# Turning activation rows with VectorE's 32x32 transpose instead of TensorE, for five experts and two token chunks of a fused attention and mixture-of-experts kernel

## The chip, the cores and the metric

The kernel runs on one core of a Trainium2 chip. The metric is the device time of one execution in microseconds (us); each time below is a median of several executions or that of the one profiled execution, as said. The engines are PE (TensorE matmul; PEld its weight loads), DVE (VectorE), ACT (ScalarE), POOL (GpSimd) and SP (SyncE, which here issues most DMAs).

## The reference

```python
def reference(...):
    y = linear_attention(q, k, v, a_re, a_im)      # complex decay, 2 x 8 heads x 768 x 48
    x = y.transpose(0, 2, 1, 3).reshape(1536, 384)
    logits = x @ w_gate                            # 8 experts, top 1
    e, gate_w = argmax(logits, 1), softmax(logits)[argmax]
    # every token goes to a slot of its expert, at most 384 slots an expert
    h = relu(disp @ w1)                            # [8, 384, 384] x [8, 384, 1024]
    z = h @ w2                                     # x [8, 1024, 384]
    x = gate_w * z[expert, slot]                   # back in token order
    g = x @ w_in                                   # 384 x 2048
    g = max(g, 0) + alpha * min(g, 0)
    return g @ w_out                               # 2048 x 384
```

## The kernel before

Three stages follow one another. The attention stage (to about 152 us) is ordered by a planner written in Python; it ends by scattering every token's row of 384 numbers to its expert's slots in a DRAM buffer `xs_d`. The expert stage (about 152 to 300 us) runs the eight experts one after the other on 256 slots each. The chunk stage (about 300 to 503 us) runs the second network over 1536 tokens in three chunks of 512. An `If` at the end, not taken for these inputs, repeats experts that hold more than 256 tokens.

Each number is carried as two parts, a high part (`xh`, `wh`, `gh`) rounded by ScalarE and a low part (`xl`, `wl`, `gl`) that VectorE takes as the difference, and each product is three matmuls (high by high, high by low, low by high). `ffn` does the two layers for an expert or a chunk. It runs over blocks `ft` of 128 hidden units: 8 for an expert, 16 for a chunk. For each it issues nine matmuls into `hp` (L1234), has ACT and DVE make `gh` and `gl`, and issues the second layer's matmuls into `y` (L1217) one or more blocks later: six for an expert's two tiles of tokens, twelve for a chunk's four. In the first block of an expert or chunk the six matmuls that read `xh` come ahead of the three that read `xl`.

The first layer needs the rows turned: 384 features on partitions, tokens along the free axis. `split_rows` does that for 128 rows: three TensorE transposes of 128x128 into one PSUM tile `pt` (L1194), then `xh` from `pt` by ACT (L1196) and `xl` by DVE (L1197). For experts 1 to 7 `gather_expert` loads the rows of the next expert from `xs_d` by two DMAs on SP (L1297) and `split_expert` turns both blocks. For the second and third chunk `combine` gathers the rows of four tiles by indirect DMAs on POOL (L1364), multiplies them by the gate (L1370) and turns them. The first chunk has a path of its own (`first_chunk`), and expert 0 too.

Work for what comes next is hung on hooks of the running `ffn`: a hook of block `ft` is called in the program after that block's `gh` and `gl`. `GA` and `HK1` say at which block rows are gathered, `GS[e]` at which block of expert e those of expert e + 1 are turned (3 in experts 1 to 6, 5 in expert 0). In a chunk gathering and turning share one hook: block 9 in the first chunk, 3 in the second. `follow` puts an instruction behind the block's last `gl` (for DVE) or its `hp` (for PE) on its own engine. The order of each engine's queue is otherwise chosen by the tile framework when it builds the program, from modelled times; every engine then runs its queue in order. Weights come in pieces: SP loads them into staging tiles, and hooks call `piece`, which makes `wh` (L359) and `wl` (L360). Buffers with the tag `rows` hold the gathered rows: four of 128x384 before. The output copies `o` of the chunks use them too.

Of the kernel before, what the change touches and what calls it, by code (L numbers as in the profile page):

```python
# [10 lines left out]
F32 = mybir.dt.float32  # L11
# [66 lines left out]
GATE = 18  # L78
BEHIND = ('A', 'AV')
GA = 1  # L80
GS = [5] + [3] * 6 + [7]
HK0 = 0
GATES_AT = 3
PAIRED = 15
# [135 lines left out]
def tile_kernel(  # L220
# [50 lines left out]
    xs_d = tc.dram_tile([NE * CAP, DM], F32, name="xs_d")  # L271
    ys_d = tc.dram_tile([NE * CAP + 1, DM], F32, name="ys_d")
    gs_d = tc.dram_tile([NE * CAP, 1], F32, name="gs_d")
    srel = cpool.tile([P, CHT], F32, name="srel")
    eidx = cpool.tile([P, CHT], U32, name="eidx")

# [25 lines left out]
    def land():  # L302
        for tag, todo in coming.items():
            while todo and busy[tag] < slots[tag]:
                kk, j0, k = todo[0]
                behind_rows = kk >= GATE or (kk == GATE - 1 and j0 >= 2)
                if (behind_rows and not first_gathers) or (kk == 3 and not second_rows):
                    break
                todo.pop(0)
                busy[tag] += 1  # L310
                src, c, n, m = shape(kk)
                rows = src[j0 * m * P:(j0 + k) * m * P, :]
                if kk >= 2 * NE:
                    st = swp.tile([P, m, n, 2], U32, tag="sw", name=f"sw{kk}", bufs=slots["sw"])
                    ins = nc.sync.dma_start(
                        out=st.rearrange("p m n w -> p m (n w)"), in_=rows.bitcast(U32).rearrange("(m p) n -> p m n", p=P)
                    )
                else:
                    p_ = stp if tag == "st" else swp
                    st = p_.tile([P, k * m, n], F32, tag=tag, name=f"st{kk}", bufs=slots[tag])  # L320
                    ins = nc.sync.dma_start(out=st, in_=rows.rearrange("(m p) n -> p m n", p=P))
# [12 lines left out]
                for j in range(k):  # L334
                    landed[kk, j0 + j] = (st[:, j * m:(j + 1) * m], tag, j == k - 1)
# [850 lines left out]
    def work(behind, limit):  # L1186
        if todo and todo[0][0] <= limit:
            piece(*todo.pop(0), behind)
        land()

    def split_rows(rows, xh, xl, j, behind=None):
# [12 lines left out]
    def ffn(xh, xl, N, units, sink, hooks, tail=None, ends="A", hold=0):  # L1204
# [67 lines left out]
        for t in range(nt):  # L1272
            if hold and t == nt - 1:
                for n, e in enumerate("VA"):
                    cs = slice(n * DM // 2, (n + 1) * DM // 2)
                    o = fp.tile([P, DM // 2], F32, tag="o", name="o", bufs=OB)
                    if e == "A":
                        A(out=o, in_=ys[t][:, cs], func=ACTF.Copy)
                    else:
                        V.tensor_copy(out=o, in_=ys[t][:, cs])  # L1280
                    sink(t, o, cs, nc.scalar if n else nc.sync)
                continue
            last_ones = len(ends) > 1
            o = fp.tile([P, DM], F32, tag="rows" if last_ones else "o", name="o", bufs=4 if last_ones else OB)
            if ends[t % len(ends)] == "A":
                A(out=o, in_=ys[t], func=ACTF.Copy)
            else:
                V.tensor_copy(out=o, in_=ys[t])
            sink(t, o)

    def gather_expert(e):
        xh = fp.tile([P, KC, SLOTS], F32R, tag="xh", name="xh")
        xl = fp.tile([P, KC, SLOTS], F32R, tag="xl", name="xl")
        rows = []
        for j in range(SLOTS // P):
            rows.append(fp.tile([P, DM], F32, tag="rows", name="rows", bufs=4))
            ins = nc.sync.dma_start(out=rows[j], in_=xs_d[e * CAP + j * P:e * CAP + (j + 1) * P, :])  # L1297
            after_scatters(ins)
            if e == 1:
                second_rows.append(ins)  # L1300
        return xh, xl, rows

    def split_expert(xh, xl, rows, behind):
        for j in range(SLOTS // P):
            split_rows(rows[j], xh, xl, j, behind)
        return xh, xl

    def fullest_expert(behind):
        ones = fp.tile([P, P], BF16, tag="rows", name="ones", bufs=4)
        cnt = fp.tile([P, NE], BF16, tag="rows", name="cnt", bufs=4)  # L1310
# [4 lines left out]
        mc = fp.tile([P, 1], F32, tag="rows", name="mc", bufs=4)  # L1315
        V.tensor_reduce(out=mc, in_=pc, axis=AX.X, op=ALU.max)
        V.tensor_copy(out=most, in_=mc)

    def overflow():
# [6 lines left out]
        with tc.If(fullest > SLOTS):  # L1326
            for e in range(NE):
                r0 = e * CAP + SLOTS
                rows = fp.tile([P, DM], F32, tag="rows", name="rows", bufs=4)
# [11 lines left out]
                for ft in range(FT):  # L1341
                    hp = pm.tile([P, P], F32, tag="h", name="hp", bufs=3)
                    for c in range(KC):
                        T.matmul(out=hp, lhsT=a1[c][:, ft * P:(ft + 1) * P], rhs=xT[:, c, :], start=(c == 0), stop=(c == KC - 1))
                    hr = fp.tile([P, P], F32, tag="gn", name="hr")
                    V.tensor_scalar(out=hr, in0=hp, scalar1=0.0, scalar2=None, op0=ALU.max)
                    a2 = fp.tile([P, DM], F32, tag="rows", name="a2", bufs=4)
                    nc.sync.dma_start(out=a2, in_=w2[e, ft * P:(ft + 1) * P, :])
                    T.matmul(out=yp, lhsT=hr, rhs=a2, start=(ft == 0), stop=(ft == FT - 1))
                o = fp.tile([P, DM], F32, tag="o", name="o", bufs=OB)  # L1350
                V.tensor_copy(out=o, in_=yp)
                nc.sync.dma_start(out=ys_d[r0:r0 + P, :], in_=o)
            for c in range(NTILE // CHT):
                ffn(*combine(c, CHT), CHT * P, [NE, NE + 1], lambda t, o, c=c: store_chunk(c, t, o), {})

    xe = (xh0, xl0)

    def combine(c, n, behind=None):
        xh = fp.tile([P, KC, n * P], F32R, tag="xh", name="xh")
        xl = fp.tile([P, KC, n * P], F32R, tag="xl", name="xl")  # L1360
        for j in range(n):
            i = c * n + j
            rows = fp.tile([P, DM], F32, tag="rows", name="rows", bufs=4)
# [55 lines left out]
    def first_chunk():  # L1419
# [4 lines left out]
        pts.append(pm.tile([P, n * P], F32, tag="tr", name="pt"))  # L1424
        got = []
        for j in range(n):
            rows = fp.tile([P, DM], F32, tag="rows", name="rows", bufs=4)
# [58 lines left out]
    for e in range(NE):  # L1486
# [11 lines left out]

        def turned(behind, e=e):
            if e + 1 < NE:  # L1500
                nxt[0] = split_expert(*nxt[0], behind)
            else:
                first_chunk_rows(behind, range(CHT // 2))

# [24 lines left out]
    for c in range(nch):  # L1529
# [52 lines left out]
```

## Time and profile before

| | |
|---|---|
| median of 3 runs | 513.21 us (512.49 to 513.21) |
| the profiled execution, whole | 511.71 us |
| its span (first to last instruction) | 509.6 us |
| granted TensorE clock, mean | 0.998 |

A row of a timeline gives start, duration, engine, line, operation, tiles and shape; `xN` at its end says that N instructions are merged, and a bracket gives the idle time of the engine ahead of it and what ended it. A matmul's duration there includes its way through the array, and matmuls overlap; what one takes of PE is the distance from its start to the next start.

### The profile page before, as it was taken

The page shows a single profiled execution, that of the slowest core. Times are in us where ns is not written, and L with a number is a line of the kernel's source. Part 1 is how long each engine was busy: PE and PEld are TensorE (multiplying, and loading weights), DVE is VectorE, ACT ScalarE, POOL GpSimd, SP SyncE. Part 2 cuts the span into 40 slices and gives each one's busy share as a digit, 9 for nine tenths or more (in the row PEclk, how much of TensorE's full clock was granted, in tenths as well). Part 3 has the DMA queues.
Part 4 walks back from the last instruction along what each step waited for, and adds up shares of the span by engine and source line. Part 5 has one row for each costly group of instructions (what it writes and reads, how often), then busy time and mean ns, then how long its engine had stood idle before and what let it go on. Part 6 is the DMA issues. An engine that isn't in the chain of part 4 may idle for free.

```text
span 509.6 us, 8757 instructions
## 1 busy us (share of the span) xinstructions
PE 496.0 (97%) x3379; PEld 452.4 (89%) x3379; DVE 343.7 (67%) x624; ACT 306.3 (60%) x566; POOL 75.0 (15%) x73
## 2 busy tenths in 40 slices
PE   7899999999999999999999999999999999999994
PEld 7778787888899999999999989999998999989984
DVE  5698999898956777767689769988354334333332
ACT  7898999989633755666663455556454344433441
POOL 0243045264431000300000330000030000000000
PEclk9999999999999999999999999999999999999999
DMA  8845789221234978859744475330030000100002
GB/s 266 274 134 172 238 282 342 87 93 41 93 127 153 381 227 292 222 177 360 268 146 150 147 271 187 131 123 1 0 125 0 1 0 1 62 2 0 1 0 68
DMA packets 38210, 71.96 MB, mean 141 GB/s; under 512 B 4777, under 2 KB 29362, under 8 KB 37394
## 3 DMA queue, kind: packets, MB, share of 16 engines
q1 hardware_dynamic: 36226, 66.12, 39.0%
q0 software_dynamic: 1792, 5.12, 3.1%
q8 instruction: 28, 0.46, 0.4%
q14 instruction: 20, 0.16, 0.1%
q10 hardware_dynamic: 144, 0.10, 0.1%
HBM read 56.76 MB, written 14.56 MB: 140 GB/s over the span
## 4 chain that ended last, share of the span: by engine, by line
PE 86%; ACT 6%; DVE 3%; DMA 2%; issue 0%; SPq 0%
PE hp L1234 32%; PE y L1217 32%; PE y L687 4%; PE sc L668 3%; PE u L701 2%; PE px L727 2%; PE pkT L648 2%; PE pt L1194 1%; PE pqT L648 1%; PE pt L560 1%; PE pl L509 1%; ACT L421 1%; PE pt L563 1%; DMA sw<-in_moe_w_out 1%; DMA ar<-in_a_re 1%; ACT w L492 1%
## 5 line engine op out<-in xcount | busy, mean ns | idle before, releaser
L1234 PE MATMUL hp<-xh,wh 128*128 128x256 f32 (+1 forms) x336 | 110.2, 330 | 0.0
L1234 PE MATMUL hp<-xh,wl 128*128 128x256 f32 (+1 forms) x336 | 109.6, 328 | 0.0
L1217 PE MATMUL y<-wh,gh 128*128 128x384 f32 x320 | 108.6, 339 | 0.0
L1217 PE MATMUL y<-wl,gh 128*128 128x384 f32 x320 | 107.7, 337 | 0.0
L1234 PE MATMUL hp<-xl,wh 128*128 128x256 f32 (+1 forms) x336 | 107.4, 330 | 0.1
L1217 PE MATMUL y<-wh,gl 128*128 128x384 f32 x320 | 91.7, 339 | 0.1
L360 DVE TENSOR_TENSOR wl<-st,wh 128x768 fp32r<-128x768 f32 (+1 forms) x63 | 67.4, 1070 | 17.5 <-ACT wh L359 16.9
L1251 DVE SCALAR_TENSOR_TENSOR gn<-gn,nalp,gp 128x512 f32<-128x512 f32 x48 | 35.9, 749 | 63.0 <-ACT gp L1250 62.1
L1249 ACT ACTIVATE gn<-hp 128x512 f32<-128x512 f32 x48 | 28.7, 598 | 81.0 <-PE hp L1234 76.5
L1234 PEld LDWEIGHTS hp<-xh,wh 128*128 128x128 f32 x336 | 63.2, 188 | 5.3 <-ACT xh L1482 0.6
L1234 PEld LDWEIGHTS hp<-xl,wh 128*128 128x128 f32 x336 | 62.2, 188 | 5.5 <-DVE xl L1483 0.6
L1234 PEld LDWEIGHTS hp<-xh,wl 128*128 128x128 f32 x336 | 63.2, 188 | 4.4
L359 ACT ACTIVATE wh<-st 128x768 fp32r<-128x768 f32 (+1 forms) x63 | 58.8, 933 | 8.1 <-DMA st<-in_moe_w 4.8
L1217 PEld LDWEIGHTS y<-wl,gh 128*128 128x128 f32 x320 | 60.2, 188 | 1.5
L1217 PEld LDWEIGHTS y<-wh,gh 128*128 128x128 f32 x320 | 60.2, 188 | 1.5
L1217 PEld LDWEIGHTS y<-wh,gl 128*128 128x128 f32 x320 | 56.8, 188 | 1.1 <-DVE gate L989 0.4
L1253 DVE TENSOR_TENSOR gl<-gn,gh 128x512 fp32r<-128x512 f32 x48 | 33.1, 691 | 29.6 <-ACT gh L1252 29.6
L1244 ACT ACTIVATE gh<-hp 128x256 fp32r<-128x256 f32 x64 | 24.5, 383 | 47.4 <-PE hp L1234 47.4
L455 POOL TENSOR_TENSOR ai<-ai 128x384 f32<-128x384 f32 x36 | 33.7, 936 | 65.8 <-ACT ai L512 64.0
L1252 ACT ACTIVATE gh<-gn 128x512 fp32r<-128x512 f32 x48 | 30.2, 629 | 19.5 <-DVE gn L1251 18.3
L1245 DVE SCALAR_TENSOR_TENSOR gl<-hp,gh 128x256 fp32r<-128x256 f32 x64 | 26.9, 421 | 13.5 <-ACT gh L1244 13.4
L1250 ACT ACTIVATE gp<-hp 128x512 f32<-128x512 f32 x48 | 28.4, 591 | 0.0
(178 smaller groups left out, 765.8 us busy)
## 6 DMA issues: line engine op xcount, KB each, us to landing
st<-in_moe_w SPq DMA_DIRECT2D x24, 512.0 KB, 3.8
st<-in_moe_w SPq DMA_DIRECT2D x12, 768.0 KB, 4.3
sw<-in_moe_w_in SPq DMA_DIRECT2D x6, 1024.0 KB
sw<-in_moe_w_out SPq DMA_DIRECT2D x8, 768.0 KB, 4.2
xs_d<-zero SPq DMA_DIRECT2D x4, 1152.0 KB
vt<-in_v SPq DMA_DIRECT2D x12, 256.0 KB
st<-in_moe_w SPq DMA_DIRECT2D x8, 384.0 KB, 3.4
ys_d<-o SPq DMA_DIRECT2D x16, 192.0 KB, 5.2
```

Of the source, the lines that this page charges most:

```text
L359: follow(A(out=wh[:, js], in_=st, func=ACTF.Copy), behind, "A")
L360: follow(V.tensor_tensor(out=wl[:, js], in0=st, in1=wh[:, js].bitcast(F32), op=ALU.subtract), behind, "V")
L455: (V if e == "V" else G).tensor_tensor(out=t, in0=t, in1=t, op=ALU.mult)
L1217: ins = T.matmul(out=ys[t], lhsT=a[:, sl], rhs=b[:, f, :], start=(ft == 0 and m == 0), stop=(ft == nf - 1 and m == 2))
L1234: ins = T.matmul(out=hp, lhsT=a[:, c, fs], rhs=b[:, c, :], start=(n == 0), stop=(n == 3 * KC - 1))
L1244: last["A"] = A(out=gh, in_=hp, func=ACTF.Relu)
L1245: last["V"] = V.scalar_tensor_tensor(out=gl, in0=hp, scalar=0.0, in1=gh.bitcast(F32), op0=ALU.max, op1=ALU.subtract)
L1249: A(out=gn, in_=hp, func=ACTF.Relu, scale=-1.0)
L1250: A(out=gp, in_=hp, func=ACTF.Relu)
L1251: V.scalar_tensor_tensor(out=gn, in0=gn, scalar=nalp[:, ft:ft + 1], in1=gp, op0=ALU.mult, op1=ALU.add)
L1252: last["A"] = A(out=gh, in_=gn, func=ACTF.Copy)
L1253: last["V"] = V.tensor_tensor(out=gl, in0=gn, in1=gh.bitcast(F32), op=ALU.subtract)
```

## The change

For experts 2 to 6 and for the second and third chunk the rows are turned by VectorE's transpose, which transposes every 32x32 block in place. The four blocks of a 128-column band must therefore already lie in the right group of 32 partitions, and the DMA that loads the rows does that. One VectorE transpose turns both 128-row blocks (128x768), one ACT instruction makes `xh` and one DVE instruction `xl`, from SBUF and not from PSUM.

For an expert (`blocked(..., True)`) four DMAs load 32 partitions each, in runs of 96 numbers (384 bytes). The 384 features are dealt out differently over the partitions for this, and the first-layer weights of these experts are loaded with rows in the same order (`first_rows`). For a chunk (`blocked(..., False)`) the gated rows are first stored to a new DRAM buffer `zs_d`, two tiles at a time, and loaded again in runs of 32 numbers (128 bytes). The `rows` tag now has two buffers of 128x2x384, the same bytes as before; `pair_tile` takes one, also for the tile that receives the transpose (`turned`).

Turning moves to block 5 of experts 1 to 5; expert 6 stays at 3. In the chunks it has a hook of its own, block 13 (`HK2`) of the first chunk and 8 of the second. Expert 1, expert 7 and the first chunk are turned by TensorE as before, and their rows come by one DMA for the pair.

```diff
-GS = [5] + [3] * 6 + [7]
+GS = [5] + [5] * 5 + [3, 7]
+DEALT = (2, 3, 4, 5, 6)
+HK2 = 13
+BLK = 32
+    def first_rows(src, k):
+        return src.rearrange("(p k) n -> k p n", k=DM // P)[k].unsqueeze(1)
...
+    def pair_tile(name):
+        return fp.tile([P, 2, DM], F32, tag="rows", name=name)
+
+    def blocked(rows, dealt):
+        b = P // BLK
+        pair = pair_tile("blocks")
+        if dealt:
+            dst = pair.rearrange("p j d -> p (j d)").rearrange("p (a d) -> p a d", d=DM // b)
+            src, turns = rows.rearrange("(a r) (b d) -> b r a d", r=BLK, b=b), dst.rearrange("p a (c k) -> p a k c", k=KC)
+        else:
+            dst = pair.rearrange("p j d -> p (j d)").rearrange("p (k a c) -> p k a c", k=KC, c=BLK)
+            src, turns = rows.rearrange("(a r) (k b c) -> b r k a c", r=BLK, b=b, c=BLK), dst
+        return turns, [nc.sync.dma_start(out=dst[n * BLK:(n + 1) * BLK], in_=src[n]) for n in range(b)]
+
+    def split_blocks(turns, dealt, xh, xl, behind=None):
+        pair = pair_tile("turned").rearrange("p j d -> p (j d)")
...
+        follow(V.transpose(out=out, in_=turns), behind and {"V": behind["low"]}, "V")
+        A(out=xh, in_=t, func=ACTF.Copy)
+        V.tensor_tensor(out=xl, in0=t, in1=xh.bitcast(F32), op=ALU.subtract)
...
     def gather_expert(e):
-        for j in range(SLOTS // P):
-            rows.append(fp.tile([P, DM], F32, tag="rows", name="rows", bufs=4))
-            ins = nc.sync.dma_start(out=rows[j], in_=xs_d[e * CAP + j * P:e * CAP + (j + 1) * P, :])
+        src = xs_d[e * CAP:e * CAP + SLOTS, :]
+        if e in DEALT:
+            rows, loads = blocked(src, True)
+        else:
+            rows = pair_tile("rows")
+            loads = [nc.sync.dma_start(out=rows, in_=src.rearrange("(j p) d -> p j d", p=P))]
...
     def combine(c, n, behind=None):
-            split_rows(rows, xh, xl, j, behind)
+            if j % 2:
+                nc.sync.dma_start(out=zs_d[(i - 1) * P:(i + 1) * P, :].rearrange("(j p) d -> p j d", p=P), in_=pair)
+
+    def split_chunk(c, n, xh, xl, behind=None):
+        for j in range(0, n, 2):
+            i, sl = c * n + j, slice(j * P, (j + 2) * P)
+            split_blocks(blocked(zs_d[i * P:(i + 2) * P, :], False)[0], False, xh[:, :, sl], xl[:, :, sl], behind)
...
+        def turned(behind, c=c):
+            split_chunk(c + 1, CHT, *nxt[0], behind)
+
+        if c + 1 < nch:
+            hooks[HK2 if c == 0 else 8].append(turned)
         hooks[HK1 if c == 0 else 3].append(ahead if c + 1 < nch else fullest_expert)
```

## Rows read from the trace of the kernel before

**Rows 1.** Page, part 1: busy us, share of the span, instructions.

```profile
PE 496.0 (97%) x3379; PEld 452.4 (89%) x3379; DVE 343.7 (67%) x624; ACT 306.3 (60%) x566; POOL 75.0 (15%) x73
```

**Rows 2.** Page, part 4: the chain that ended last, by engine.

```profile
PE 86%; ACT 6%; DVE 3%; DMA 2%; issue 0%; SPq 0%
```

**Rows 3.** Windows: length, busy time (instructions) by engine, PE clock, DMA share, GB/s.

```profile
210.00:220.00 10.00, 10.00 (x74) 10.00 (x74) 6.55 (x11) 5.85 (x12) 2.57 (x3) 1.00 0.69 157
...
260.00:270.00 10.00, 10.00 (x71) 10.00 (x70) 10.00 (x15) 5.80 (x12) 0.00 (x0) 1.00 0.48 159
270.00:280.00 10.00, 10.00 (x76) 9.84 (x76) 10.00 (x19) 3.91 (x8) 0.00 (x0) 1.00 0.36 114
...
360.00:380.00 20.00, 20.00 (x104) 17.97 (x103) 9.94 (x16) 11.11 (x21) 3.86 (x4) 1.00 0.19 62
```

**Rows 4.** Timeline of PE around one block's transposes in expert 4.

```profile
235.42 0.49 PE L1194 MATMUL pt<-ident,rows 128*128 128x128 f32 x3
235.66 0.42 PE L1217 MATMUL y<-wh,gh 128*128 128x384 f32 x1
235.92 0.34 PE L1217 MATMUL y<-wl,gh 128*128 128x384 f32 x1
236.10 0.34 PE L1217 MATMUL y<-wh,gl 128*128 128x384 f32 x1
```

**Rows 5.** Line L1194: durations in ns (min/median/max), first and last start.

```profile
L1194 PE MATMUL pt<-ident,rows x66: 270/272/275, 163.4 to 403.9; 128*128 128x128 f32 x66
```

**Rows 6.** Groups by form: count | busy us, mean ns | idle us before, releaser.

```profile
L360 DVE TENSOR_TENSOR wl<-st,wh 128x768 fp32r<-128x768 f32 x36 | 34.4, 955 | 11.2 <-ACT wh L359 10.8 <-issue 0.3
L359 ACT ACTIVATE wh<-st 128x768 fp32r<-128x768 f32 x36 | 30.3, 842 | 7.2 <-DMA st<-in_moe_w 4.8 <-DVE st L356 2.4
L1197 DVE TENSOR_TENSOR xl<-pt,xh 128x384 fp32r<-128x384 f32 x22 | 12.1, 551 | 0.5 <-ACT xh L1196 0.5
L1196 ACT ACTIVATE xh<-pt 128x384 fp32r<-128x384 f32 x22 | 10.8, 489 | 2.6 <-PE pt L1194 2.6
L349 DVE TENSOR_SCALAR st<-sw 128x768 uint32<-128x768 uint32 x8 | 4.5, 561 | 0.6 <-DMA sw<-in_moe_w_out 0.6
```

**Rows 7.** Timelines of DVE (block 5 of expert 2), PE (first block of expert 3).

```profile
199.87 0.43 DVE L1245 SCALAR_TENSOR_TENSOR gl<-hp,gh 128x256 fp32r<-128x256 f32 x1 [0.42 <-ACT gh L1244]
...
203.81 0.28 PE L1234 MATMUL hp<-xh,wh 128*128 128x256 f32 x1
...
204.52 0.52 PE L1234 MATMUL hp<-xl,wh 128*128 128x256 f32 x3
```

**Rows 8.** Timelines of DVE (gating; block 13 of chunk 1), PE (chunk 2 begins).

```profile
341.87 1.40 DVE L1370 TENSOR_SCALAR rows<-rows,gate 128x384 f32<-128x384 f32 x4
355.08 0.69 DVE L1253 TENSOR_TENSOR gl<-gn,gh 128x512 fp32r<-128x512 f32 x1 [0.70 <-ACT gh L1252]
...
365.98 0.39 PE L1234 MATMUL hp<-xh,wh 128*128 128x512 f32 x1
...
367.37 0.85 PE L1234 MATMUL hp<-xl,wh 128*128 128x512 f32 x3
```

**Rows 9.** DMA view, window 25.5 to 26 us: packets; the queue's share.

```profile
DMA packets 388, 0.15 MB, mean 298 GB/s; under 512 B 387, under 2 KB 387, under 8 KB 388
q1 hardware_dynamic: 388, 0.15, 111.4%
```

**Rows 10.** DMA view, whole run: issues, KB each, median us to landing.

```profile
rows<-xs_d SPq DMA_DIRECT2D x14, 192.0 KB, 7.0
...
out<-o SPq DMA_DIRECT2D x11, 192.0 KB, 1.9
```

**Rows 11.** Timeline of SP: one load of an expert's rows.

```profile
195.22 0.32 SPq L1297 DMA_DIRECT2D rows<-xs_d  x1
```

**Rows 12.** Timeline of DVE in expert 7: gating the first chunk's rows.

```profile
288.75 0.42 DVE L1439 TENSOR_SCALAR rows<-rows,gate 128x384 f32<-128x384 f32 x1 [1.82 <-DMA rows<-ys_d,eidx]
```

More of the change, by code (lines that the diff above doesn't have):

```diff
@@ L273, in tile_kernel @@
     gs_d = tc.dram_tile([NE * CAP, 1], F32, name="gs_d")
+    zs_d = tc.dram_tile([NTILE * P, DM], F32, name="zs_d")
     srel = cpool.tile([P, CHT], F32, name="srel")
@@ L311, in land @@
                 src, c, n, m = shape(kk)
-                rows = src[j0 * m * P:(j0 + k) * m * P, :]
+                rows = src[j0 * m * P:(j0 + k) * m * P, :].rearrange("(m p) n -> p m n", p=P)
+                if kk % 2 == 0 and kk // 2 in DEALT:
+                    rows = first_rows(src, j0)
                 if kk >= 2 * NE:
@@ L315, in land @@
                     ins = nc.sync.dma_start(
-                        out=st.rearrange("p m n w -> p m (n w)"), in_=rows.bitcast(U32).rearrange("(m p) n -> p m n", p=P)
+                        out=st.rearrange("p m n w -> p m (n w)"), in_=rows.bitcast(U32)
                     )
@@ L320, in land @@
                     st = p_.tile([P, k * m, n], F32, tag=tag, name=f"st{kk}", bufs=slots[tag])
-                    ins = nc.sync.dma_start(out=st, in_=rows.rearrange("(m p) n -> p m n", p=P))
+                    ins = nc.sync.dma_start(out=st, in_=rows)
                 if behind_rows:
@@ L1189, in work @@
         land()
+    def pair_tile(name):
[12 more added lines that the diff above has]
+        pair = pair_tile("turned").rearrange("p j d -> p (j d)")
+        if dealt:
+            out = pair.rearrange("p (a k r) -> p a k r", k=KC, r=BLK)
+            t = out.rearrange("p a k r -> p k a r")
+            xh, xl = (x.rearrange("p k (a r) -> p k a r", r=BLK) for x in (xh, xl))
+        else:
+            out, turns = pair, turns.rearrange("p k a c -> p (k a c)")
+            t = pair.rearrange("p (k t) -> p k t", k=KC)
+        follow(V.transpose(out=out, in_=turns), behind and {"V": behind["low"]}, "V")
+        A(out=xh, in_=t, func=ACTF.Copy)
+        V.tensor_tensor(out=xl, in0=t, in1=xh.bitcast(F32), op=ALU.subtract)
     def split_rows(rows, xh, xl, j, behind=None):
@@ L1282, in ffn @@
                 continue
-            last_ones = len(ends) > 1
-            o = fp.tile([P, DM], F32, tag="rows" if last_ones else "o", name="o", bufs=4 if last_ones else OB)
+            if len(ends) > 1:
+                if t % 2 == 0:
+                    pair = pair_tile("o")
+                o = pair[:, t % 2]
+            else:
+                o = fp.tile([P, DM], F32, tag="o", name="o", bufs=OB)
             if ends[t % len(ends)] == "A":
@@ L1293, in gather_expert, with split_expert @@
         xl = fp.tile([P, KC, SLOTS], F32R, tag="xl", name="xl")
-        rows = []
-        for j in range(SLOTS // P):
-            rows.append(fp.tile([P, DM], F32, tag="rows", name="rows", bufs=4))
-            ins = nc.sync.dma_start(out=rows[j], in_=xs_d[e * CAP + j * P:e * CAP + (j + 1) * P, :])
+        src = xs_d[e * CAP:e * CAP + SLOTS, :]
+        if e in DEALT:
+            rows, loads = blocked(src, True)
+        else:
+            rows = pair_tile("rows")
+            loads = [nc.sync.dma_start(out=rows, in_=src.rearrange("(j p) d -> p j d", p=P))]
+        for ins in loads:
             after_scatters(ins)
-            if e == 1:
-                second_rows.append(ins)
+        if e == 1:
+            second_rows.extend(loads)
         return xh, xl, rows
-    def split_expert(xh, xl, rows, behind):
-        for j in range(SLOTS // P):
-            split_rows(rows[j], xh, xl, j, behind)
+    def split_expert(e, xh, xl, rows, behind):
+        if e in DEALT:
+            split_blocks(rows, True, xh, xl, behind)
+        else:
+            for j in range(SLOTS // P):
+                split_rows(rows[:, j], xh, xl, j, behind)
         return xh, xl
     def fullest_expert(behind):
-        ones = fp.tile([P, P], BF16, tag="rows", name="ones", bufs=4)
-        cnt = fp.tile([P, NE], BF16, tag="rows", name="cnt", bufs=4)
+        ones = fp.tile([P, P], BF16, tag="rows", name="ones")
+        cnt = fp.tile([P, NE], BF16, tag="rows", name="cnt")
         pc = pm.tile([P, NE], F32, tag="tr", name="pc")
@@ L1314, in fullest_expert @@
         follow(T.matmul(out=pc, lhsT=ones, rhs=cnt, start=True, stop=True), behind, "h")
-        mc = fp.tile([P, 1], F32, tag="rows", name="mc", bufs=4)
+        mc = fp.tile([P, 1], F32, tag="gsl", name="mc", bufs=1)
         V.tensor_reduce(out=mc, in_=pc, axis=AX.X, op=ALU.max)
@@ L1328, in overflow @@
                 r0 = e * CAP + SLOTS
-                rows = fp.tile([P, DM], F32, tag="rows", name="rows", bufs=4)
+                rows = fp.tile([P, DM], F32, tag="rows", name="rows")
                 after_scatters(nc.sync.dma_start(out=rows, in_=xs_d[r0:r0 + P, :]))
@@ L1346, in overflow @@
                     V.tensor_scalar(out=hr, in0=hp, scalar1=0.0, scalar2=None, op0=ALU.max)
-                    a2 = fp.tile([P, DM], F32, tag="rows", name="a2", bufs=4)
+                    a2 = fp.tile([P, DM], F32, tag="rows", name="a2")
                     nc.sync.dma_start(out=a2, in_=w2[e, ft * P:(ft + 1) * P, :])
@@ L1353, in overflow @@
             for c in range(NTILE // CHT):
-                ffn(*combine(c, CHT), CHT * P, [NE, NE + 1], lambda t, o, c=c: store_chunk(c, t, o), {})
+                ffn(*split_chunk(c, CHT, *combine(c, CHT)), CHT * P, [NE, NE + 1], lambda t, o, c=c: store_chunk(c, t, o), {})
     xe = (xh0, xl0)
@@ L1362, in combine @@
             i = c * n + j
-            rows = fp.tile([P, DM], F32, tag="rows", name="rows", bufs=4)
+            if j % 2 == 0:
+                pair = pair_tile("rows")
+            rows = pair[:, j % 2]
             ins = G.indirect_dma_start(
@@ L1426, in first_chunk @@
         for j in range(n):
-            rows = fp.tile([P, DM], F32, tag="rows", name="rows", bufs=4)
+            if j % 2 == 0:
+                pair = pair_tile("rows")
+            rows = pair[:, j % 2]
             ins = G.indirect_dma_start(
@@ L1500, in turned @@
             if e + 1 < NE:
-                nxt[0] = split_expert(*nxt[0], behind)
+                nxt[0] = split_expert(e + 1, *nxt[0], behind)
             else:
```

1 line of the change is left out of this document (added).

## The prediction

> **What bounds the kernel now.** I read the page's busy times first. PE is busy 496.0 of 509.6 us, DVE 343.7 [rows 1]. Busy PE time holds overlap and alone proves little, so the chain of waits comes next: 86% of the span is on PE [rows 2], and from 152 to 290 us and again from 302 to 503 us it hardly leaves PE. The windows by stage agree: in the middle of the experts (210 to 220 us) PE is busy 10.00 of 10 us and DVE 6.55; in the chunks (360 to 380) PE 20.00 of 20, DVE 9.94 [rows 3]. The granted clock is 1.00 in all of these, the 2.4 GHz level, so nothing is to be had or lost there. One stretch has two full engines: from 260 to 280 us DVE is busy 10.00 of 10 twice [rows 3]. Last I read starts in the timeline of PE, since a matmul's own duration (272 ns for one transpose, [rows 5]) counts its way through the array. What the reader is to see: PE runs from one matmul straight into the next, so a matmul taken out is worth its distance to the next start, wherever nothing else becomes late.
>
> **What is removed.** 66 transposes run on line L1194 [rows 5], three for each of 22 blocks of 128 rows. The change takes away those of experts 2 to 6 (5 x 2 blocks) and of two chunks (2 x 4 blocks): 18 threes. Their price: a three starts at 235.42, and two `y` matmuls later a start is at 236.10; an undisturbed step from `y` to `y` is 0.18 there (235.92 to 236.10), 0.175 over a longer run. 0.68 - 2 x 0.175 = 0.33 us [rows 4]. The distances of the other threes that I looked at, between `hp` matmuls and in the chunks, give 0.32 to 0.335. So 18 x 0.33 = 5.9 us of PE time, 3.3 in the experts and 2.6 in the chunks. This is the gain, if PE stays without a gap.
>
> **What is added on DVE and ACT.** For each pair of blocks DVE gets one 128x768 transpose, T. The trace has no such operation. Nearest below is a 128x768 DVE instruction of 0.561 us, nearest above I take two passes of the 0.955 us that a subtraction of 128x768 takes: 1.9 us [rows 6]. I take T = 0.955: every element passes once, as in the subtraction, and no row shows 0.561 for anything but a shift. `xh` by ACT becomes one instruction of 0.842 for two of 0.489, `xl` one of 0.955 for two of 0.551 [rows 6]. Net for a pair: DVE +0.81 us, ACT -0.14. That is 9 x 0.81 = 7.3 us on DVE, hidden by its idle time (35% and 50% of the windows of 210 and 360 us, [rows 3]) as long as no one waits for the result.
>
> The Trainium skill, VectorE: DVE Perf Modes, section The three transpose paths, measures 311 ns for 128 columns of bf16 in 32x32 blocks, which as an estimate is 6 x 311 = 1.87 us for this T, and its Rules for kernel authors send a 128x128 transpose to TensorE where PSUM will do. No run here shows a VectorE transpose; by that figure the case is the rival of a slow T below, at 510.7 us.
>
> **Who waits for T: the experts.** T stands behind `gl` of block 5. For expert 3 that `gl` ran from 199.87 to 200.30 [rows 7]. Then T to 201.25, `xh` to 202.2, `xl` to 203.3 (0.1 us for each handover, my allowance). The first `hp` of expert 3 read `xh` at 203.81 and `xl` at 204.52 [rows 7]; one three (0.33) leaves PE in between, so the limits are 203.48 and 204.19. Slack 0.9 us; if a `wl` of 0.955 [rows 6] slips in on DVE, about nothing. Queued behind T on DVE are that `wl` and `gl` of block 6, for which only `y` of block 6 waits, a block later. Cost taken: 0, bounds 0 and 5 x 0.95 = 4.8 us (five experts, each late by one more pass).
>
> **Who waits for T: the chunks.** The second chunk's rows are gated at 341.87 [rows 8], so store and first load have until 355.8; two tiles of output take 1.9 us to land, rows from `xs_d` 7.0 at worst [rows 10]: 9 of 14 us. With two buffers the second load can only start when the first T has read its block. `gl` of block 13 ends at 355.8 [rows 8], T to 356.7, four issues of 0.32 [rows 11], landing 1.9 to 7.0 us later [rows 10]: 359.9 to 365.0; then T, `xh`, `xl`: done between 362.7 and 367.8, `xh` 1.0 before. The chunk's first matmuls read `xh` at 365.98 and `xl` at 367.37 [rows 8], 0.66 earlier without two threes. Late by nothing or by 1.5 us; I take 0. The third chunk turns at block 8 of 16, some 33 us ahead.
>
> **What is added on DMA.** An expert's rows come in 1024 packets of 384 bytes for 256 of 1536, a chunk pair in 3072 of 128. In half a microsecond of small packets (387 of 388 under 512 bytes, 390 on average) the queue moved 298 GB/s, 1.114 x 0.5 x 16 / 388 = 23 ns a packet [rows 9]. So an expert's rows take 1024 x 23 / 16 = 1.5 us of all engines, and a chunk pair 1.3 us (by bytes) to 4.4 us (if 128 bytes cost what 384 do), inside the 1.9 to 7.0 above. An expert's load is issued some 12 us before its T. Two more issues on SP, 0.64 us an expert [rows 11], stand ahead of weight loads, which wait for staging buffers anyway. From 338 us to the first output store SP has nothing else to issue, and POOL's gathers keep their place. The weights in the new order still come in rows of 4 KB. Cost taken: 0; without that cover 0.5 us an expert (1.5 against 1.0).
>
> The Trainium skill, DMA: Bandwidth & Descriptors, Specifications, wants at least 512 bytes a transfer for line rate and names a read-modify-write below. The 298 GB/s of [rows 9] disagree for 384-byte reads into SBUF. Were small packets to cost twice as much, the second load of the second chunk would land up to 4.4 us later than its middle, 362.5; its low part, done at 365.3 against 366.7 then, would be 3.0 us late, and the sum would be 510.8 us.
>
> **The full DVE stretch.** Expert 6 is turned just ahead of 260 to 283 us, where DVE has no idle time. If that backlog of `wl` and unpacking work, and not PE, set when expert 7's last steps run, PE's lead of 3.3 us would shrink there: DVE's next idle time is 1.82 us at 288.75 [rows 12], so at most 3.3 + 0.8 - 1.8 = 2.3 us go. Its bottom is 0, because the stretch starts when weights arrive in buffers that PE's progress sets free. I take 0.5.
>
> **Sum.** -5.9 + 0.5 = -5.4 us. The profiled execution took 511.7 us (span 509.6 and 2.1 around it), which gives 506.3; the median of the runs is 1.5 us above it, so the forecast is 513.2 - 5.4 = 507.8 us.
>
> **Rivals.** (a) Part of the gain goes. Either the DVE stretch takes the whole of the experts' 3.3 us, so that only the chunks' 2.6 stay: 510.6 us. For it speaks DVE's 10.00 of 10, against it that PE shows no gap in the same windows [rows 3]. Or T takes 1.9 us: the experts lose 0.2 to 4.8 us and the second chunk, with two T in its chain, about 0.9; 1.2 to 5.7, in the middle 3.4, gives 513.2 - 5.9 + 3.4 = 510.7 us. (b) Slower: T is slower than two passes. Each expert is late by T - 0.95 - 0.9, the second chunk by 2 (T - 0.95) less a slack of 1.0 (the middle of 3.6 and -1.5). 5 (T - 1.85) + 2 (T - 0.95) - 1.0 passes 5.9 at T = 2.6 us; three passes, 2.9 us, lose 8.2 and give 515.5 us. Nothing in the profile prices T, but no DVE row of this shape is over one pass. (c) The change does nothing that can be seen: PE's freed slots turn into waits of equal length, because the queue orders are rebuilt from modelled times and a T that stands ahead of its load holds up `gl`. 513.2 us. Against it: the waits on DVE and ACT before block 6 leave 0.9 us in each expert and PE has spare `y` work to go on with. (d) More gain than removed: the new order also closes some of the waits between 290 and 302 us, 1 us or so: 506.3.
>
> **How the numbers follow.** The forecast's case (506.8 to 509, where the lost part is 0 to 1.7 us) has 0.58, (a) 0.20, (b) 0.08, (c) 0.06, (d) 0.08. A measurement of this kernel can tell 0.2%, 1.0 us, from no change. Faster are the forecast, (d) and all of (a): 0.86; same is (c): 0.06; slower (b): 0.08. The range goes from (d), less 0.8 us for the spread of the runs (513.21 against 512.49), 505.5, to 511.5, which holds (a) with 0.8 us above it. What is left out is (b), (c) and the far end of a slow T.
>
> **What would show it.** Right: 12 transposes left on L1194, PE's chain without a gap, T near 0.95 us, the `y` and `hp` starts at the same distances, stores of the experts some 3.3 us earlier after expert 5, and the second and third chunk 1.3 us shorter each. Wrong in T: its mean in the groups by form, with PE's weight load waiting for DVE `xl` at the starts of experts 2 to 6. Wrong in the chunks: `hp` waiting for `xl` at the start of the second chunk, behind a DMA into `blocks`. Wrong in the DVE stretch: expert 7 as late as before. The prediction fails as a whole if T is above 2.6 us or if DVE's queue stands before a load that has not landed.

## The result, and the profile after

The changed kernel takes 507.26 us (median of five runs, 505.98 to 508.51) against 513.21 (511.96 to 513.49) for the kernel before beside it. The ratio is 0.9892, 95% interval 0.9867 to 0.9916, so 1.1% faster. Its profiled execution took 506.6 us with a span of 504.4: 5.1 us less than that of before.

Part 1 of the page of the changed kernel, to be read against [rows 1]:

```profile
PE 490.3 (97%) x3325; PEld 446.9 (89%) x3325; DVE 350.6 (70%) x624; ACT 304.8 (60%) x557; POOL 74.5 (15%) x73
```

PE has 54 instructions and 5.7 us less, DVE 6.9 us more. The groups by form of VectorE, ScalarE and TensorE show the new instructions, and the transposes that are left on TensorE; the last two rows are the view by source line of the transpose and of its loads (durations in ns, min/median/max):

```profile
L1223 DVE STREAM_TRANSPOSE turned<-blocks 128x768 f32<-128x768 f32 x9 | 10.0, 1114 | 2.3 <-DMA blocks<-zs_d 2.3
L1225 DVE TENSOR_TENSOR xl<-turned,xh 128x768 fp32r<-128x768 f32 x9 | 8.6, 960 | 1.4 <-ACT xh L1224 1.3
L1224 ACT ACTIVATE xh<-turned 128x768 fp32r<-128x768 f32 x9 | 7.6, 846 | 7.0 <-DVE turned L1223 7.0
L1230 PE MATMUL pt<-ident,rows 128*128 128x128 f32 x12 | 2.1, 272 | 0.0
...
L1223 DVE STREAM_TRANSPOSE turned<-blocks x9: 972/1222/1230, 182.5 to 406.9; 128x768 f32<-128x768 f32 x9
...
L1212 SPq DMA_DIRECT2D blocks<-zs_d x16: 557/646/687, 342.4 to 403.6; - x16
```

T has two durations: 0.97 us in the four transposes of the chunks and 1.22 in the five of the experts. The windows that [rows 3] give for before (length, busy time and instructions of PE, PEld, DVE, ACT and POOL, PE clock, DMA share, GB/s):

```profile
210.00:220.00 10.00, 10.00 (x72) 10.00 (x71) 7.14 (x11) 6.50 (x11) 0.99 (x2) 1.00 0.98 186
260.00:270.00 10.00, 9.92 (x71) 9.68 (x70) 10.00 (x17) 5.58 (x13) 0.00 (x0) 1.00 0.29 88
270.00:280.00 10.00, 10.00 (x76) 9.56 (x75) 8.82 (x16) 3.96 (x9) 0.00 (x0) 1.00 0.52 202
360.00:380.00 20.00, 20.00 (x103) 18.26 (x102) 9.94 (x17) 9.69 (x18) 4.33 (x4) 1.00 0.30 93
```

PE is still full, with 0.08 us of gap in one window. The chain of waits, though, leaves PE for DVE, ACT and a weight load from 247 to 266 us. Its line by engine, to be read against [rows 2], and some pieces of that stretch (start, length, what):

```profile
PE 77%; ACT 9%; DVE 5%; issue 4%; DMA 3%; POOL 1%; SPq 0%; POOLq 0%; DVEq 0%
...
250.28 0.71 DVE turned L1223
...
252.55 5.74 DMA st<-in_moe_w
...
262.90 0.87 DVE wl L369
263.77 2.27 DVE st L362 x2
266.04 0.35 DVE gl L1281
...
266.43 1.34 PE y L1253 x6
```

This is where expert 6 is turned: `y` now waits for a `gl` that stands behind weight and unpacking work on DVE.

To place the gain I mark, in PE's timelines, the first `hp<-xl,wh` matmul of the first expert and of each chunk (for the second chunk of before it is the 367.37 of [rows 8]). **E** is from the first expert to the first chunk, **C1** from the first chunk to the second, **C2** from the second to the third; from there to the last output tile both kernels take 68.0 us. Each is read from one profiled execution.

| kernel | E | C1 | C2 | ratio (95%) |
|---|---|---|---|---|
| before | 147.44 | 66.53 | 67.89 | |
| after | 144.61 | 64.98 | 66.58 | 0.9892 (0.9867 to 0.9916) |
| experts alone | 144.98 | 66.36 | 67.89 | 0.9939 (0.9919 to 0.996) |
| chunks alone | 147.68 | 65.08 | 66.58 | 0.9967 (0.9951 to 0.9982) |
| idle transposes | 147.45 | 66.47 | 67.89 | 1.0 (0.9985 to 1.0015) |
| expert 7 too | 145.03 | 64.99 | 66.58 | 0.9914 (0.9892 to 0.9936) |
| T issued twice | 148.33 | 70.29 | 65.21 | 1.0039 (1.0022 to 1.0055) |
| without expert 6 | 144.80 | 65.16 | 66.57 | 0.9908 (0.9894 to 0.9923) |
| short runs | 144.94 | 64.98 | 66.58 | 0.9908 (0.9894 to 0.9922) |
| short runs, expert 1 too | 146.06 | 65.02 | 66.58 | 0.9963 (0.9948 to 0.9978) |
| T and a half | 146.31 | 66.51 | 65.17 | 0.9933 (0.9906 to 0.996) |
| block 6 | 146.90 | 64.98 | 66.58 | 0.9931 (0.9909 to 0.9953) |
| block 15 | 144.15 | 75.75 | 65.95 | 1.0072 (1.005 to 1.0094) |

From before to after E falls by 2.83, C1 by 1.55 and C2 by 1.31: 5.69 us.

### The profile page after: what moved, and what is told of

Read it like the earlier page. It is cut to its first block, busy times and chain, and to the rows that moved or that the text cites. A ratio compares the mean times of both kernels' runs of the same rounds, so it can differ in the third digit from the quotient of the medians.

```text
span 504.4 us, 8694 instructions
## 1 busy us (share of the span) xinstructions
PE 490.3 (97%) x3325; PEld 446.9 (89%) x3325; DVE 350.6 (70%) x624; ACT 304.8 (60%) x557; POOL 74.5 (15%) x73
## 2 busy tenths in 40 slices
DMA packets 55811, 75.12 MB, mean 149 GB/s; under 512 B 22633, under 2 KB 46962, under 8 KB 54994
## 3 DMA queue, kind: packets, MB, share of 16 engines
q1 hardware_dynamic: 53826, 69.27, 44.5%
## 4 chain that ended last, share of the span: by engine, by line
PE 77%; ACT 9%; DVE 5%; issue 4%; DMA 3%; POOL 1%; SPq 0%; POOLq 0%; DVEq 0%
PE y L1253 31%; PE hp L1270 31%; PE y L696 2%; PE sc L677 2%; ACT L430 2%; PE u L710 2%; PE pt L569 1%; DMA st<-in_moe_w 1%; PE pqT L657 1%; PE pkT L657 1%; PE px L736 1%; PE pl L518 1%; ACT ar L462 1%; PE pt L572 1%; POOL xs_d L883 1%
## 5 line engine op out<-in xcount | busy, mean ns | idle before, releaser
L1253 PE MATMUL y<-wh,gl 128*128 128x384 f32 x320 | 89.5, 339 | 0.1
```

The lines of the kernel that those rows point to most:

```text
L1253: ins = T.matmul(out=ys[t], lhsT=a[:, sl], rhs=b[:, f, :], start=(ft == 0 and m == 0), stop=(ft == nf - 1 and m == 2))
```

## The experiments

**Each half alone.** For the experts alone, the chunks go back to `split_rows`:

```diff
-ffn(*split_chunk(c, CHT, *combine(c, CHT)), ...)
+ffn(*combine(c, CHT), ...)
...
-            if j % 2:
-                nc.sync.dma_start(out=zs_d[...], in_=pair)
+            split_rows(rows, xh, xl, j, behind)
...
-        if c + 1 < nch:
-            hooks[HK2 if c == 0 else 8].append(turned)
```

> Only experts 2 to 6 are turned by VectorE; the two later chunks by TensorE as before. If the gain is PE time at 0.33 us for each three of transposes, less 0.5 us in the stretch where DVE is full, this is 10 x 0.33 - 0.5 = 2.8 us faster than before (ratio 0.9945). If the experts' part is lost in that stretch, 0 to 1 us (ratio 0.998 to 1.0). If the gain comes from new queue orders as a whole, no share can be foretold and e1 and e2 need not add up to the 5.5 us of the whole change.

For the chunks alone, no expert is dealt out:

```diff
-GS = [5] + [5] * 5 + [3, 7]
-DEALT = (2, 3, 4, 5, 6)
+GS = [5] + [3] * 6 + [7]
+DEALT = ()
```

> Only the second and third chunk are turned by VectorE; all experts by TensorE at block 3 as before. PE time alone: 8 x 0.33 = 2.6 us faster than before (ratio 0.9949), with the starts of the second and third chunk 1.3 us closer each to the start before them. If the second load from zs_d came too late for the second chunk, only about 1 us (ratio 0.998).

Medians 509.96 and 510.80 us beside 512.82 (here and below, the kernel before, run along with them). Each half moves its own stages and leaves the other's within 0.25 us of before, so the two gains add. The whole time of the chunks alone shows about 1 us less than its stages: its profiled execution ends 7.4 us after the start of the last output tile's work, that of before 6.3.

**Idle transposes.** TensorE gets the removed 54 transposes back, into a PSUM tile that nobody reads; VectorE's stay:

```diff
+        for _ in range(2 if behind else 0):
+            pt = pm.tile([P, KC, P], F32, tag="tr", name="pt")
+            for c in range(KC):
+                follow(T.transpose(pt[:, c, :], xh0[:, c, 0:P].bitcast(F32), ident), behind, "h")
```

> The changed kernel, and beside each VectorE transpose two threes of TensorE transposes of a tile that is always there, whose result nobody reads: 54 in all, as many as the change removed. If the gain is their PE time, it goes back by 18 x 0.33 = 5.9 us and the kernel is as before, ratio 0.998 to 1.002. If the gain comes from queue orders, buffers or loads, it stays near the changed kernel's 0.9892.

512.26 us, and all three stages return to those of before within 0.06 us. The gain is the PE time of 18 threes. ScalarE's shorter work, the new loads and the later places, which all stay in this kernel, are worth nothing by themselves.

**Around the full DVE stretch.** `DEALT` gets expert 7 as well, or loses expert 6:

```diff
-DEALT = (2, 3, 4, 5, 6)
+DEALT = (2, 3, 4, 5, 6, 7)
```

> The changed kernel with expert 7 turned by VectorE too, at block 3 of expert 6 as before, inside the stretch where DVE has no idle time. PE time alone: 0.66 us faster than the changed kernel. If DVE sets the pace in that stretch, its 0.8 to 1.1 us more work there cost as much: 0 to 1 us slower than the changed kernel, with more of PE's weight loads waiting for gl in expert 6.

```diff
-GS = [5] + [5] * 5 + [3, 7]
-DEALT = (2, 3, 4, 5, 6)
+GS = [5] + [5] * 4 + [3, 3, 7]
+DEALT = (2, 3, 4, 5)
```

> The changed kernel with expert 6 turned by TensorE at block 3 of expert 5, as before: DVE has 1.1 us less to do just ahead of the stretch in which it is full, PE 0.66 us more. If that stretch takes 0.5 us through this T, the two nearly cancel: within 0.3 us of the changed kernel. If the stretch does not care, 0.66 us slower.

508.33 us (beside 512.82) and 507.36 (beside 511.88): neither can be told from the changed kernel by its interval. In E, four experts give 2.64 us, just 4 x 0.66; five give 2.83, six 2.41. That fits a stretch in which DVE, and not PE, sets the pace, but E alone doesn't prove it: three other kernels that turn the same five experts at the same blocks (experts alone, short runs, block 15) have 144.98, 144.94 and 144.15. Another sign is `gl` of the last block of experts 6 and 7 in DVE's timeline. It runs 3.04 and 2.12 us earlier than before in the changed kernel, 2.22 and 1.42 in the experts alone, 2.74 and 1.52 with short runs, 4.44 and 1.74 in the kernel that turns the second chunk at block 15, but 3.07 and 2.94 where expert 6 stays on TensorE. With expert 6 turned, expert 7 loses 0.8 to 2.7 us of this lead, without it 0.13. E does not show the loss: 2.64 us are gained without expert 6, 2.46 to 3.29 with it.

**A slower T.** The transpose is issued again, whole or in half, before it counts:

```diff
+        for _ in range(2 if behind else 1):        # 4 in the second kernel
-        follow(V.transpose(out=out, in_=turns), behind and {"V": behind["low"]}, "V")
+            follow(V.transpose(out=out, in_=turns), behind and {"V": behind["low"]}, "V")
```

> The changed kernel with every VectorE transpose issued twice, into the same tile: T of 1.22 becomes 2.4 us for the experts, 0.97 becomes 1.9 for the chunks. By the prediction's slack of 0.9 us from a T of 0.955, each expert is late by 2.4 - 1.85 = 0.6 us and the second chunk by about 0.9: 3.8 us slower than the changed kernel. If the queue order gives way (PE takes y matmuls first) it is within 1 us of the changed kernel.

> The same with four issues: 4.9 us for the experts, 3.9 for the chunks. By the prediction's formula the experts lose 5 x (4.9 - 1.85) = 15 us and the second chunk 5: slower than before by 14 us. If the order gives way up to the 6.3 us of PE work that lie between block 5 and the next expert, less: 3 to 8 us slower than the changed kernel, so about level with before.

```diff
+        if behind:
+            half = slice(0, 4) if dealt else slice(0, DM)
+            follow(V.transpose(out=out[:, half], in_=turns[:, half]), {"V": behind["low"]}, "V")
```

> The changed kernel with half of every VectorE transpose issued again: T of 1.22 becomes 1.8 us in the experts, 0.97 becomes 1.5 in the chunks. The slack by the prediction (T up to 1.85 us costs nothing) says 0 to 0.5 us slower than the changed kernel. If the slack is used up already at the T of the changed kernel, as the doubled T suggests (7.5 us for twice), about half of that, 3 to 4 us slower.

508.34 us for one and a half (beside 511.94), 513.96 for two and 544.71 for four (both beside 511.88). Each is off its expectation: by the ratios, one and a half is 2.1 us slower than the changed kernel, between the two cases, two is 7.5 slower for 3.8, and four is 32.8 slower than before.

In the experts these kernels do more than lengthen T. DVE in expert 1 of T twice:

```profile
182.92 1.23 DVE L1224 STREAM_TRANSPOSE turned<-blocks 128x768 f32<-128x768 f32 x1
184.05 0.93 DVE L369 TENSOR_TENSOR wl<-st,wh 128x768 fp32r<-128x768 f32 x1
184.89 1.24 DVE L1224 STREAM_TRANSPOSE turned<-blocks 128x768 f32<-128x768 f32 x1
...
188.41 0.96 DVE L1226 TENSOR_TENSOR xl<-turned,xh 128x768 fp32r<-128x768 f32 x1
```

A `wl` stands between the two issues, and two `gl` and two `wl` behind them. `xl` is done 6.45 us after the first issue starts, where the changed kernel has 3.10 (182.51 to 185.61) and the second issue adds 1.24. One and a half has the same order. So what E loses in these kernels is the price of a longer T and of a later place of `xl` together; no run here parts them. In the second chunk the issues of T twice stand back to back.

The waits of T twice (who waited for whom: us, times, longest), PE where its second chunk begins, and the windows after it:

```profile
PEld hp L1271 <- ACT xh L1225: 3.4, 2, 2.4
PEld hp L1271 <- DVE xl L1226: 3.2, 4, 1.4
...
367.93 0.50 PE L1271 MATMUL hp<-xh,wh 128*128 128x512 f32 x1 [2.10 <-ACT xh L1225]
...
368.00:370.00 2.00, 2.00 (x7) 1.63 (x8) 1.47 (x2) 0.40 (x1) 0.00 (x0) 0.74 0.00 0
370.00:372.00 2.00, 2.00 (x8) 2.00 (x7) 0.00 (x0) 0.00 (x0) 0.00 (x0) 0.50 0.00 0
372.00:374.00 2.00, 2.00 (x10) 1.69 (x10) 0.00 (x0) 0.67 (x2) 0.00 (x0) 0.91 0.00 0
```

With T twice E grows by 3.7 us over the changed kernel, where the prediction's 5(T - 1.85) makes 3.0 at T = 2.44; C1 and C2 together by 3.9, where 2(T - 0.95) - 1.0 makes 1.0. (With T and a half E grows by 1.70 for 5(1.92 - 1.85) = 0.35, C1 and C2 by 0.13 for 0.2.) The 3.9 can be followed. Two T add 2.0, and the second comes 6.6 us after the end of the first for 5.15 in the changed kernel, 1.4 more; less a slack of 1.3 that is the 2.1 us of PE's wait. Then PE works at a lower granted clock, down to 0.50 (the 1.2 GHz level): 2 x (0.26 + 0.50 + 0.09) = 1.7 us in the three windows.

The 1.4 us do not come from the later T. With T and a half the second T follows 5.06 us behind the end of the first; without expert 6 turned, where T is not longer, it is 6.64 (353.44 to 360.08). DVE in T twice and without expert 6, and the DMA view of T twice from 362.8 to 363.8 us:

```profile
365.01 1.99 DVE L1224 STREAM_TRANSPOSE turned<-blocks 128x768 f32<-128x768 f32 x2 [4.02 <-DMA blocks<-zs_d]
...
360.08 0.98 DVE L1223 STREAM_TRANSPOSE turned<-blocks 128x768 f32<-128x768 f32 x1 [3.05 <-DMA blocks<-zs_d]
...
q8 instruction: 1, 0.02, 5.9%
```

In both kernels one packet of the instruction queue q8 falls inside the load; here it takes 0.059 x 16 = 0.94 us of an engine, and the load's last 11 packets come only after 363.75, as it ends; the load is done 0.9 us later after its last issue than in the changed kernel, which is most of the 1.4. In the changed kernel the load is done (358.24) before the q8 packet starts (358.30). That the one holds up the other is read from these times, not tested.

With four T the first two views show more of the waits and of the clock:

```profile
PE hp L1271 <- ACT xh L1225: 20.0, 6, 3.6
...
210.00:220.00 10.00, 6.53 (x31) 6.21 (x30) 6.34 (x8) 4.38 (x7) 1.33 (x1) 0.66 0.71 210
```

The span is 37.9 us longer than the changed kernel's for 3 x (5 x 1.22 + 4 x 0.97) = 30 us of DVE time: PE stands still for 20 us behind `xh` alone, and the clock is at 0.66 in the middle of the experts. A result this late costs more than the time added to T.

**A later place.** Turning moves to block 6 of experts 1 to 5, or to block 15 in the first chunk:

```diff
-GS = [5] + [5] * 5 + [3, 7]
+GS = [5] + [6] * 5 + [3, 7]
```

> The changed kernel with the experts turned one block later (block 6 of 8 for experts 2 to 6): the same work, 2.1 us later. By a slack of 0.9 us each of five experts starts 1.2 us late: 6 us slower than the changed kernel. If PE's queue is built with y matmuls of the old expert ahead of the new one's hp where the rows come late, as between experts 0 and 1, 0 to 1.5 us slower: then it is DVE work that costs in the runs with a longer T, and not lateness.

```diff
-HK2 = 13
+HK2 = 15
```

> The changed kernel with the second chunk turned at block 15 of 16 for 13. The same chain of two loads and two transposes (9.0 us in the changed kernel) then starts 8.4 us later, some 7 us too late for the second chunk: 4 to 7 us slower than the changed kernel if the chain is what counts; 0 to 1 us if the framework starts the transposes earlier all the same or PE finds other work.

508.86 and 516.13 us (beside 511.94). Block 6 costs E 2.3 us, 0.46 an expert, against a block's 2.1, and lies between the two cases of its expectation: PE, whose order is rebuilt around the later block, has other work for most of that time and waits 1.4 us for `xl` in three experts. At block 15 nothing is left to put in between, and the loss passes the 4 to 7 us expected. PE in that kernel, its waiting row with two `hp` behind it, DVE's second T, and the windows:

```profile
370.84 0.79 PE L1270 MATMUL hp<-xh,wh 128*128 128x512 f32 x1 [6.29 <-ACT xh L1224]
371.43 0.63 PE L1270 MATMUL hp<-xh,wl 128*128 128x512 f32 x1
371.86 0.63 PE L1270 MATMUL hp<-xh,wh 128*128 128x512 f32 x1
...
368.93 0.98 DVE L1223 STREAM_TRANSPOSE turned<-blocks 128x768 f32<-128x768 f32 x1 [3.33 <-DMA blocks<-zs_d]
...
372.00:374.00 2.00, 2.00 (x7) 1.52 (x6) 0.44 (x1) 0.36 (x1) 0.02 (x1) 0.50 0.67 241
374.00:376.00 2.00, 2.00 (x6) 1.61 (x5) 0.00 (x0) 0.92 (x2) 1.70 (x2) 0.50 0.35 94
376.00:378.00 2.00, 2.00 (x9) 1.54 (x8) 1.10 (x2) 0.83 (x3) 1.52 (x2) 0.84 0.50 160
```

The chain is the one that the prediction drew (first T, buffer free, load, second T, `xh`), and it ends 6.3 us late. The rest of the loss is the clock: starts of `hp` lie 0.43 us apart at 0.50, where the changed kernel has 0.23 at 1.00, and 13 of them at 0.2 us more make 2.6 us. That is 8.9 of the 10.77 - 0.63 = 10.1 us by which C1 and C2 grew; another 0.57 is a wait of `y` for `gh` at 362.17, and 0.6 us stay unplaced.

**Short runs, and expert 1.** The experts' rows come in 128-byte runs as the chunks' do, with the weights in plain order; then expert 1 is turned too:

```diff
-            rows, loads = blocked(src, True)
+            rows, loads = blocked(src, False)
...
-            split_blocks(rows, True, xh, xl, behind)
+            split_blocks(rows, False, xh, xl, behind)
...
-                if kk % 2 == 0 and kk // 2 in DEALT:
-                    rows = first_rows(src, j0)
```

> The changed kernel with the experts' rows loaded as the chunks' are, in runs of 128 bytes (3072 packets for 1024), and the weights in plain row order; T then reads its block with a stride of one element, not three. Expected: T falls from 1.22 to 0.97 us in the experts, 1.25 us less DVE work in all. If packets of 128 bytes cost what 384 do (23 ns), the DMA engines have 2.9 us more for each expert, in a stretch where they are 75 to 100% busy, and weights come late: 1 to 4 us slower. If small packets cost by their bytes, equal or up to 0.5 us faster.

```diff
-DEALT = (2, 3, 4, 5, 6)
+DEALT = (1, 2, 3, 4, 5, 6)
```

> The variant with runs of 128 bytes and plain weight order, and expert 1 turned by VectorE too, at block 5 of expert 0, where DVE is busy little more than half of the time. PE time at 0.33 us a three: 0.66 us faster than that variant (ratio to before 0.9895 for its 0.9908), all of it between the starts of experts 0 and 1. If the four loads of expert 1 make weights late while the DMA engines are full (160 to 180 us), no gain or 1 us slower.

Short runs: 507.22 us (beside 511.88), level with the changed kernel. The view by source line of the transpose and the DMA part of the page, with 10,240 packets more than the 55,811 of the changed kernel (whose q1 has 44.5%):

```profile
L1221 DVE STREAM_TRANSPOSE turned<-blocks x9: 967/969/979, 182.8 to 406.9; 128x768 f32<-128x768 f32 x9
...
DMA packets 66051, 75.12 MB, mean 149 GB/s; under 512 B 32873, under 2 KB 57202, under 8 KB 65234
...
q1 hardware_dynamic: 64066, 69.27, 45.1%
```

T is 0.97 in all nine, so the 1.22 came from the way its source was read: with 384-byte runs the features of a group lie three numbers apart in `blocks`, with 128-byte runs side by side. The 0.25 us saved on each T show in no time. For the packets: the 0.6% of 16 engines over 504.6 us is 48 us, 9.7 an expert. What one of 128 bytes takes can be read where the changed kernel loads the second chunk's second pair: from 353 to 360 us the DMA view has 3136 packets on q1 with 35.7% of 16 engines, 13 ns each, where by bytes, from 23 for 384 [rows 9], it would be 8. Cheap, but not free, and hidden here.

With expert 1: 510.24 us (beside 511.94), by the ratios 2.8 us slower than with short runs alone, where 0.66 were to be won and 1 to be lost at most. The profiled execution, 508.38 us, is the fastest of the ten; its E is 1.12 us longer than with short runs alone, so the trace places only part of the loss. ScalarE and PE in expert 1, and the windows of that kernel from 160 to 164 us:

```profile
168.68 0.84 ACT L366 ACTIVATE wh<-st 128x768 fp32r<-128x768 f32 x1 [4.63 <-DMA st<-in_moe_w]
169.42 0.83 ACT L1222 ACTIVATE xh<-turned 128x768 fp32r<-128x768 f32 x1
...
170.30 0.39 PE L1268 MATMUL hp<-xh,wh 128*128 128x256 f32 x1 [2.10 <-ACT xh L1222]
...
160.00:162.00 2.00, 2.00 (x16) 2.00 (x15) 1.46 (x3) 0.38 (x1) 0.00 (x0) 1.00 0.64 98
162.00:164.00 2.00, 2.00 (x17) 2.00 (x16) 0.39 (x1) 0.34 (x1) 0.00 (x0) 1.00 0.89 124
```

and the same two windows with short runs alone:

```profile
160.00:162.00 2.00, 2.00 (x17) 2.00 (x16) 1.49 (x3) 0.37 (x1) 0.00 (x0) 1.00 0.99 348
162.00:164.00 2.00, 1.90 (x15) 1.70 (x14) 0.42 (x1) 0.28 (x2) 0.00 (x0) 1.00 1.04 348
```

There 348 GB/s of weights come in; with expert 1 turned its four row loads go first, 98 and 124 GB/s pass, and the `wh` that started at 166.08 starts at 168.68. T itself was done at 165.7. But `xh` stands on ScalarE behind that `wh`, and PE waits 2.10 us for it. This is the kind of loss that the prediction priced at 0.5 us for a load whose cover is gone; it is larger, and it ends on PE by way of a third queue.

## Why the prediction was right, point by point

**The price of a three: right.** 0.33 us was read from starts [rows 4]. C2 fell by 1.31 = 4 x 0.33, and putting the idle transposes back undid all of it.

**T: right in the chunks, low in the experts.** 0.955 was taken; 0.97 and 1.22 were measured. The missing term is the read at a distance of three numbers, 0.25 us. DVE's busy time rose by 6.9 us for the 7.3 foretold, but that they lie so near is luck: the rows add 10.0 + 8.6 - 18 x 0.551 = 8.7 us of work, and busy time counts overlapping instructions once (T starts at 182.51, the `gl` ahead of it runs until 182.59). By the Trainium skill, VectorE: DVE Perf Modes, section The three transpose paths, T was estimated at 1.87 us; the trace does not agree, at 0.97 to 1.22 for a 128x768 of fp32, so the slow-T form of rival (a) fell with it.

**Who waits in the experts: right that nobody does, for a reason half seen.** DVE and PE between experts 1 and 2, to be read against [rows 7]:

```profile
182.17 0.42 DVE L1281 SCALAR_TENSOR_TENSOR gl<-hp,gh 128x256 fp32r<-128x256 f32 x1 [0.78 <-ACT gh L1280]
182.51 1.22 DVE L1223 STREAM_TRANSPOSE turned<-blocks 128x768 f32<-128x768 f32 x1
183.65 0.92 DVE L369 TENSOR_TENSOR wl<-st,wh 128x768 fp32r<-128x768 f32 x1
184.65 0.96 DVE L1225 TENSOR_TENSOR xl<-turned,xh 128x768 fp32r<-128x768 f32 x1
...
185.79 0.28 PE L1270 MATMUL hp<-xh,wh 128*128 128x256 f32 x1
...
187.20 0.52 PE L1270 MATMUL hp<-xl,wh 128*128 128x256 f32 x3
```

A `wl` did slip in and T was longer, which by the prediction leaves no slack; still `xl` is done at 185.61 for a first reader at 187.20. The rebuilt order puts four `y` between the readers of `xh` and of `xl`, 1.41 us apart where it was 0.71. In experts 3 to 6 `xl` is done 2.7, 1.3, 1.5 and 1.1 us ahead of its reader. The margin is not large: with T and a half, where `xl` also stands further back, PE waits for it in two experts (0.27 and 0.55 us).

**The second chunk: right in its ending, with one step mis-sized.** DVE, ACT and PE there, for [rows 8]:

```profile
352.58 0.97 DVE L1223 STREAM_TRANSPOSE turned<-blocks 128x768 f32<-128x768 f32 x1
...
358.70 0.98 DVE L1223 STREAM_TRANSPOSE turned<-blocks 128x768 f32<-128x768 f32 x1 [1.56 <-DMA blocks<-zs_d]
...
359.71 0.85 ACT L1224 ACTIVATE xh<-turned 128x768 fp32r<-128x768 f32 x1 [3.44 <-DVE turned L1223]
...
361.82 0.39 PE L1270 MATMUL hp<-xh,wh 128*128 128x512 f32 x1
```

The second T waits for its load as foretold, `xh` is done at 360.56 and is read at 361.82: 1.3 us of slack, 1.7 for `xl`. The four issues were put at 0.32 each [rows 11]; they take 0.65, which the landing, at the short end of 1.9 to 7.0, gave back.

**DMA: right for this change, because it was covered.** The stages leave no room for a cost, and shorter runs still changed nothing that can be told. At 13 ns for 128 bytes the prediction's range of 1.3 to 4.4 us for a chunk pair becomes 3072 x 13 / 16 = 2.5. Expert 1 shows the cost where weights are waited for. The Trainium skill, DMA: Bandwidth & Descriptors, section Specifications, wants 512 bytes for line rate: 128-byte runs fall behind line rate (98 and 124 GB/s), while the 298 GB/s of [rows 9] were moved in runs of 384. How much of the lower rate is the packets' is open: SP's four issues of that load take 3.36 us (158.58 to 161.94), and the engines are 64 to 89% busy.

**The full DVE stretch: place shown, size left open.** 0.5 was taken out of 0 to 2.3. E gave 2.83 of 3.3, but the same five experts gave 2.46, 2.50 and 3.29 in other kernels, so 0 to 0.8 us is what the runs bear. That the chain would stay on PE was wrong: it leaves PE from 247 to 266 us, and PE shows only 0.08 us of gap there.

**The sum.** Foretold -5.4 us, profiled -5.1, medians -5.95. Rivals (c) and (d) fell with the stages: the gain is as large as what was removed, and not larger. By its own terms the lower end of the forecast's case is 513.2 - 5.9 = 507.3 us, not 506.8.

**Rival (b): its point of decision was not tested cleanly.** T = 2.6 us was to be the break-even. With T twice (2.44 in the experts, 1.94 in the chunks) the kernel is already slower than before, ratio 1.0039. One thing was missing from the formula: a PE that has waited can run on at a lower clock (1.7 us). But 1.4 us of the wait that came before it lie in a load that was late by itself, and in the experts `xl` was placed further back as well. Whether one instruction of 2.44 us would have lost the gain, no run here shows.

## What to carry to other kernels

Where TensorE is full, price its transposes by the distance between starts and give them to an engine with idle time; the test is to put the same transposes back where nobody reads them. Then look at every consumer of the new result in its own queue: a result that is ready early still comes late behind an instruction that waits for something else, as with expert 1. Stop moving work where the helping engine has no idle time left: turning expert 7 as well, and turning expert 6 at all, brought nothing that could be measured. And a run that lengthens one instruction may also reorder the queue around it: read the order before the time is put down to the length.

## What the runs showed of the hardware that was not expected

- A VectorE transpose of 128x768 in fp32 takes 0.97 us from numbers that lie side by side and 1.22 from numbers 12 bytes apart. The Trainium skill, SBUF — State Buffer, section Door 1: The DMA port swizzle, wants two or more accesses to a 16-byte line for full speed and puts a penalty on each step into a new line. The trace agrees in its direction: at 12 bytes three steps of four go into a new line, and the transpose took 0.25 us longer.
- A DMA's issue on SP grows with its packets: 0.33 us (median) for 128 packets of 1536 bytes in the kernel before, 0.44 for 256 of 384 bytes and 0.65 for 768 of 128 bytes in the changed kernel. A load in runs of 128 bytes moved 98 to 124 GB/s with the DMA engines 64 to 89% busy, at most 16 ns a packet (0.77 x 4 us x 16 / 3072; 13 ns in the second chunk), where weights moved at 348.
- After a wait of 6.29 us PE's granted clock was 0.50 until about 376 us, some 5 us of work; after one of 2.10 us at the start of a chunk it fell to 0.50 as well, but after 2.10 us in expert 1 it stayed at 1.00. What tells these two apart no run here shows.
